# A long convolution by Fourier transforms: 32-bit pair copies of x on VectorE ahead of the first transform

## The chip, the core and the metric

The kernel runs on one core of a Trainium2 chip. The core has five engines, each with its own instruction queue: TensorE (PE; its weight loads are listed apart as PEld), VectorE (DVE), ScalarE (ACT), GpSimd (POOL) and SyncE (SP, which here only issues DMAs). They share an on-chip memory of 128 partitions (SBUF) and an accumulator memory (PSUM) that TensorE writes to. The metric is the device time of one execution in microseconds. A profile of one execution gives every instruction's start and duration.

## The reference

Inputs are x (8 x 5696 x 128), a filter h (5696 x 128) and four weight matrices. The first part is a causal convolution of every channel with its own filter, by real Fourier transforms of twice the length; the second mixes tokens and channels.

```python
Xf = np.fft.rfft(x, n=2*S, axis=1)
Hf = np.fft.rfft(h, n=2*S, axis=0)
y  = np.fft.irfft(Xf * Hf[None], n=2*S, axis=1)[:, :S, :]
theta = y @ w_theta
zr, zi = y * np.cos(theta), y * np.sin(theta)
u = y + einsum('ts,bsd->btd', w_tok_r, zr) + einsum('ts,bsd->btd', w_tok_i, zi)
out = u + np.maximum(u @ w_ch, 0.0)
```

The kernel's transforms work in float16.

## The kernel before

**Two parts.** The convolution takes the first 420 us or so; the token mixing, large matrix products with weights streamed in and transposed by VectorE (L714, L1099), takes the rest. The change lies in the first part alone.

**The transforms.** The length 11392 is split as 178 x 64, a sequence as 89 x 64. x of two batches sits in one tile `x16` (L125): partition = one of 89 blocks of 64 time steps, and within a partition 2 batches x 64 steps x 128 channels of float16, channels innermost. So the 128 values (2 x 64) of one channel lie 256 bytes apart. There are eight groups (L369): four pairs of batches, each in two halves `dh` of 64 channels. A group passes through four stages, all on TensorE, whose results are drained from PSUM by another engine:

- Stage A (L185 to L202), the first transform, one channel at a time. The weights that are loaded are the 89 x 128 values of the channel, `lhs(q)`, and the moving operand is a table of 89 x 180. Four channels make a chunk (one PSUM buffer); ScalarE drains it (L201) into the tile `a_`. A group has 16 chunks A.
- Stage B (L294 to L316): `f2` multiplies with the table `w_t2` (L212), ScalarE converts (L310, `xs`), and VectorE multiplies with the filter's spectrum twice (L312, into `u_t` and `v_t`). 12 chunks. In the last one, `f2` also issues 12 matmuls that no result needs (L218), into the same PSUM buffer.
- Stage C (L318 to L337): 16 matmuls a chunk, weights from `u_t` and `v_t` (L328, L329). VectorE drains the first half of a group's chunks and every second one of the rest (L336, into `g_`), ScalarE the others (L333, L334). 16 chunks. Each chunk reads all frequencies, so the first C of a group needs the last L312.
- Stage D (L339 to L366): back to time (L351), ScalarE drains (L354).

**What runs beside what.** `woven` (L222) merges lists of chunks by a position between 0 and 1 (L615): the 16 chunks C of a group are interleaved with the 16 chunks A of the next. Where the next group is the second half of the same batch pair (dh 1), the A lie in the first 0.35, three A to a C; where it is a new pair (dh 0), they lie in the first 0.55, one or two A to a C. Then come B of the next group and D of this one, interleaved (L621). All chunks take their PSUM buffer from one ring of four (L95), in program order, so that a chunk can start only when the fourth chunk before it has been drained. `x16` has one buffer: the load of the next pair (L130, 16 DMAs from GpSimd's queue) starts when the last A of the present one has read it.

**The first group.** Before it, tables are built on GpSimd (L150, L152), VectorE (L155, L156, L163, L182) and ScalarE (sines, L160, L167), among them `w_t2`, beside the transform of h, whose weights come from a tile `h16` with 128 bytes between values. The A of group 0 run alone, while the same engines build `r_u`, `r_v`, `sgn` and `e_t`.

**Order.** Each engine runs its instructions in the order that a scheduler fixed when the program was built; it can move an instruction ahead of others written earlier, where its tiles allow that.

Of the kernel before, what the change touches and what calls it, by code (L numbers as in the profile page):

```python
# [10 lines left out]
F32 = mybir.dt.float32  # L11
BF16 = mybir.dt.bfloat16
F16 = mybir.dt.float16
add = mybir.AluOpType.add
mult = mybir.AluOpType.mult
AF = mybir.ActivationFunctionType
ALU = mybir.AluOpType
# [5 lines left out]
def kernel(  # L23
# [10 lines left out]
    nc = tc.nc  # L34
    B, S, D = x.shape
    assert D == 128
    P = 128
# [39 lines left out]
    N2 = 64  # L77
    N1 = NF // N2
    NB = S // N2
    K1 = N1 // 2 + 1  # L80
    CK = 8
    HD = D // 2
# [7 lines left out]
    UVW = 2 * HD * K1  # L90
    hf_hbm = nc.dram_tensor("hf_hbm", (2, NCK, N2, 2, HD * CK), F16, kind="Internal").ap()
    yt_hbm = nc.dram_tensor("yt_hbm", (D, B, S), BF16, kind="Internal").ap()
# [4 lines left out]
    def psum():  # L97
        return fp.tile([P, 2, 512], F32, tag="ps", name="ps")

    conv, setup, xa, xin, pha = (ExitStack() for _ in range(5))  # L100

    def pool(name, bufs, stack, **kw):
        return stack.enter_context(tc.tile_pool(name=name, bufs=bufs, **kw))

    fa = pool("fft_a", 1, xa)
    fh = pool("fft_h", 4, xa)
    fx = pool("fft_x", 1, xin)
    NE, WB, BT = 9, 6 * 4 * CJ * 64, 7 * 1024
    keep = pool("keep", 1, ctx, side="right")
    fc = pool("fft_c", 1, conv, side="right")  # L110
# [3 lines left out]

    u_t = fc.tile([P, UVW + P], F16)
    v_t = fc.tile([P, UVW + P], F16)
    uv = [t[:, :UVW].rearrange("p (e d k) -> p e d k", e=2, k=K1) for t in (u_t, v_t)]
    h16 = s1.tile([P, 2, N2, HD], F16)
    for p0, p1 in ((0, 80), (80, NB)):
# [4 lines left out]
    def load_x(bp):  # L124
        x16 = fx.tile([P, 2, N2, D], F16, tag="x16", name="x16")  # L125
        for e in range(2):
            src = x[2 * bp + e]
            for n0 in range(0, N2, 16):
                for p0, p1 in ((0, 80), (80, NB)):
                    nc.gpsimd.dma_start(  # L130
                        x16[p0:p1, e, n0:n0 + 16, :].rearrange("p n d -> p (n d)"),
                        bass.AP(tensor=src.tensor, offset=src.offset + (p0 * N2 + n0) * D,
                                ap=[[N2 * D, p1 - p0], [1, 16 * D]]))
        return x16
# [8 lines left out]
    def turns_of(pattern, base, lanes, m, per, quarter=None):  # L143

        n = 1
        for _, c in pattern:
            n *= c
        t = s2.tile([P, 11 * NB], F32, tag="turn", name="turn")[:m, :n]
        k = s2.tile([P, 11 * NB], F32, tag="whole", name="whole")[:m, :n]
        nc.gpsimd.iota(k, pattern=pattern, base=base, channel_multiplier=0,  # L150
                       allow_small_or_imprecise_dtypes=True)
        nc.gpsimd.tensor_scalar(t, k, lanes, 1.0 / per, op0=mult, op1=mult)  # L152
        if quarter is not None:
            quarter(t)
        nc.vector.tensor_scalar(k, t, MAGIC, None, op0=add)  # L155
        nc.vector.scalar_tensor_tensor(t, k, MAGIC, t, op0=ALU.subtract, op1=ALU.subtract)  # L156
        return t, k
# [10 lines left out]

    f1_t = fc.tile([P, 2 * K1], F16)
    t, k = turns_of([[1, K1]], 0, lane[:NB, 1:2], NB, N1)  # L170
# [14 lines left out]
    def stage_a(lhs, both=False):  # L185

        st = {}

        def chunk(q):
            if q == 0:  # L190
                st["a"] = fa.tile([P, 2 * K1, HD], F16, tag="a", name="a_")
            ps = psum()
            for i in range(4):
                nc.tensor.matmul(ps[:, i // 2, (i % 2) * 2 * K1:(i % 2 + 1) * 2 * K1], lhs(q + i), f1_t[:NB],  # L194
                                 start=True, stop=True)
            a_out = st["a"][:, :, q:q + 4].rearrange("p k (a q) -> p k a q", a=2)
            a_in = ps[:, :, :4 * K1].rearrange("p a (q k) -> p k a q", q=2)
            if both and q % 8:
                nc.vector.tensor_copy(a_out, a_in)
            else:  # L200
                nc.scalar.activation(a_out, a_in, AF.Copy)  # L201
        return [lambda q=q: chunk(q) for q in range(0, HD, 4)], st  # L202
# [30 lines left out]
    x16s = {0: load_x(0)}  # L233
    steps, a_h = stage_a(lambda q: h16[:NB].rearrange("p h n d -> p (h n) d")[:, :, q], True)
# [59 lines left out]
    def stage_b(a_st, dh):  # L294

        hs_of = {}

        def load(c):
            if c >= NCK:
                return  # L300
            hs = hs_of[c] = fh.tile([P, 2, HD * CK], F16, tag="hs", name="hs")
            for e in range(2):
                nc.sync.dma_start(hs[64 * e:64 * e + 64], hf_hbm[dh, c])

        def chunk(c):
            c0, ck = CHK[c]
            hv = hs_of[c].rearrange("p r (d k) -> p r d k", k=CK)
            ps = f2(a_st, c)
            xs = fs.tile([P, 2, HD, CK], F16, tag="xs", name="xs")
            nc.scalar.activation(xs[:, :, :, :ck], ps, AF.Copy)  # L310
            for r in range(2):
                nc.vector.tensor_tensor(  # L312
                    uv[r][:, :, :, c0:c0 + ck], xs[:, :, :, :ck],
                    hv[:, r:r + 1, :, :ck].to_broadcast([P, 2, HD, ck]), op=mult)
            load(c + LEAD)
        return [lambda c=c: load(c) for c in range(LEAD)], [lambda c=c: chunk(c) for c in range(NCK)]  # L316
# [54 lines left out]
    def front(g):  # L371
        if g >= len(groups):
            return [], [], []
        bp, dh = groups[g]
        x16 = x16s[bp].rearrange("p b n d -> p (b n) d")
        steps, a_st = stage_a(lambda q: x16[:NB, :, dh * HD + q])
        return (steps, *stage_b(a_st, dh))

    a0, load0, b0 = front(0)
    woven(a0, [lambda: r_table(0, r_u), lambda: r_table(1, r_v), s_table] + load0)  # L380
    woven(b0, [lambda n0=n0: e_table(n0) for n0 in range(0, EN, 11)])
# [220 lines left out]
    for g, (bp, dh) in enumerate(groups):  # L602
        st = {}
        last = g + 1 == len(groups)
        a_, load_, b_ = front(g + 1)
        if last:
            for _ in range(3):
                steps0.pop(0)()
        now = [with_load(steps0.pop(0), n < 6) for n in range(9)] if last else []
        c_ = stage_c(st, last)  # L610
        if dh == 0 and bp + 1 < B // 2:
            def next_x(bp=bp):
                x16s[bp + 1] = load_x(bp + 1)
            a_ = a_ + [next_x]
        woven((c_, 0.06 if a_ else 0.0, 1.0), (a_, 0.0, 0.35 if dh == 0 else 0.55), now, load_)  # L615
        if g + 2 == len(groups):
            xin.close()
            open_phases()
            load_ya0()
        now = [steps0.pop(0) for _ in range(5)] if last else []  # L620
        woven(b_, (stage_d(st, bp, dh, load_ya1 if last else None), 0.0, 1.1 if b_ else 1.0), now)  # L621
        if g + 2 == len(groups):
            load_ya1()
            open_ring()
# [56 lines left out]
    bp = cp = wlp = ybp = None  # L681
# [248 lines left out]
    for i, (k, p, tt, j0, s0, nj) in enumerate(stretches):  # L930
# [38 lines left out]
        if tt is None:  # L969
            if p:  # L970
                aside(True, False)
            if first_of_pair:
                q = M1 if p else M3
# [4 lines left out]
            for j in range(nj):  # L978
                jj = j0 + s0 + j
                for r in range(2):  # L980
                    b = [x[:, r, :] for x in bts[jj]]
# [12 lines left out]
            if end_of_pair:  # L994
# [5 lines left out]
                c, c0 = c_last  # L1000
# [161 lines left out]
```

## Time and profile before

| | |
|---|---|
| Median of three runs | 2102.5 us (2101.66 to 2104.44) |
| The profiled execution | 2099.89 us |
| Its span, first to last instruction | 2098.1 us |
| Mean granted clock of TensorE | 0.978 |

Times below are within the span. The busy times of the first stages, from the table of busy time by stretch, in us:

| Stretch | What runs | PE | DVE | ACT | clock |
|---|---|---|---|---|---|
| 0 to 54.5 | tables, transform of h | 24.2 | 38.2 | 26.9 | 0.85 |
| 54.5 to 66.1 | A of group 0 | 9.5 | 9.1 | 10.9 | 0.79 |
| 66.1 to 88.4 | B of group 0 | 16.3 | 21.3 | 20.2 | 0.64 |
| 88.4 to 110.4 | C of group 0, A of group 1 | 22.0 | 14.2 | 14.4 | 0.92 |
| 110.4 to 131.1 | B of group 1, D of group 0 | 16.3 | 16.9 | 18.0 | 1.00 |
| 131.1 to 152.4 | C of group 1, A of group 2 | 21.2 | 14.4 | 17.6 | 1.00 |
| 345.5 to 368.5 | C of group 6, A of group 7 | 22.9 | 14.2 | 15.2 | 0.86 |
| 520 to 2098 | token mixing | 1547.9 | 1211.6 | 289.4 | 1.00 |

A row of the groups of instructions reads: line, engine, operation, what is written <- what is read, size, count | busy us in total, mean ns of one | idle us of the engine just before them and what ended most of it. A row of the timeline reads: start, duration, engine, line, operation, tiles, sizes, count, and in brackets the idle time before it with what ended it. Matmuls overlap each other, so their spacing, not their duration, is their cost.

### The profile page before, as it was taken

How to read it: one execution, taken by the hardware profiler on the slowest of the kernel's cores; microseconds unless marked ns; L12 is line 12 of the kernel's file. 1: busy time of each engine (PE TensorE's matmuls, PEld its weight loads, DVE VectorE, ACT ScalarE, POOL GpSimd, SP SyncE). 2: the span in 40 equal slices, each digit the busy share in tenths (PEclk: the TensorE clock that was granted, in tenths of full speed). 3: DMA queues.
4: the chain of work that ended last, by engine and by line, in shares of the span. 5: the costliest groups of instructions: out<-in, count | busy, mean ns of one | idle time of the engine just before them, and what ended most of it. 6: DMA issues, size and time to landing. Idle time of an engine off the chain costs nothing.

```text
span 2098.1 us, 41505 instructions
## 1 busy us (share of the span) xinstructions
PE 1979.5 (94%) x15688; PEld 1109.4 (53%) x15865; DVE 1595.2 (76%) x2881; ACT 675.3 (32%) x995; POOL 912.5 (43%) x1662
## 2 busy tenths in 40 slices
PE   4888999878999999999999999899999999999998
PEld 3788888754444444444444444344444444444444
DVE  7777776776878888888886766886777777777867
ACT  5887877874332333333310000011111111111111
POOL 5301010327444636354557554435354545445450
PEclk8799999989999999999999999999999999999999
DMA  7357474989989989898999989869797887879693
GB/s 144 94 137 175 123 171 121 239 243 239 179 153 179 178 175 168 171 173 177 171 175 152 154 167 284 136 107 156 127 154 132 148 142 136 154 130 155 126 155 89
DMA packets 408233, 334.97 MB, mean 160 GB/s; under 512 B 85895, under 2 KB 358407, under 8 KB 407047
## 3 DMA queue, kind: packets, MB, share of 16 engines
q0 software_dynamic: 225952, 156.72, 52.8%
q1 hardware_dynamic: 176096, 164.05, 27.3%
q10 hardware_dynamic: 5984, 11.54, 1.6%
q8 instruction: 124, 2.03, 0.4%
q14 instruction: 77, 0.63, 0.1%
HBM read 377.11 MB, written 92.49 MB: 224 GB/s over the span
## 4 chain that ended last, share of the span: by engine, by line
PE 63%; DVE 4%; DMA 2%; issue 2%; POOL 0%; ACT 0%; DVEq 0%
PE m L1099 59%; DVE c L1106 2%; DMA ring<-in_moe_w_tok_r_dram 1%; DVE b L655 1%; PE v L801 1%; PE utp L794 1%; PE m L1103 1%; DVE wt L714 1%; PE tpz L742 0%; PE theta_ps L396 0%; POOL ring L509 0%; PE m L986 0%; DMA yT<-yt_hbm 0%; PE m L1020 0%; DMA zl<-zl_hbm 0%
## 5 line engine op out<-in xcount | busy, mean ns | idle before, releaser
L509 POOL DMA_DIRECT2D ring<-in_moe_w_tok_i_dram x720 | 390.8, 557 | 653.0 <-DVE wt L714 579.6
L509 POOL DMA_DIRECT2D ring<-in_moe_w_tok_r_dram x720 | 389.0, 559 | 145.8 <-DVE wt L714 85.5
L714 DVE STREAM_TRANSPOSE wt<-ring 128x384 f32<-128x384 f32 (+2 forms) x720 | 359.3, 523 | 110.3 <-PE m L1099 70.0
L1099 PE MATMUL m<-b,wt 128*128 128x512 bf16 x1599 | 385.9, 380 | 4.1 <-DVE wt L714 1.7
L1099 PEld LDWEIGHTS <-wt 128*128 128x128 bf16 x1804 | 176.4, 98 | 219.7 <-DVE wt L714 7.8
L1106 DVE TENSOR_TENSOR c<-c,m 128x512 f32<-128x512 f32 x412 | 265.2, 669 | 0.4 <-PE m L1099 0.4
L796 ACT ACTIVATE ring<-utp 128x512 bf16<-128x512 bf16 x85 | 50.8, 597 | 582.3 <-PE utp L794 582.3
L328 PE MATMUL ps<-r_u,u_t 128*128 128x128 f16 x1024 | 126.4, 223 | 6.4 <-ACT red L419 3.0
L329 PE MATMUL ps<-r_v,v_t 128*128 128x128 f16 x1024 | 125.5, 223 | 0.4
L1020 PE MATMUL m<-b,wt 128*128 128x512 bf16 x466 | 110.2, 381 | 8.9 <-DMA b<-z_hbm 4.9
L791 ACT ACTIVATE ub<-c 128x512 bf16<-128x512 f32 x88 | 55.0, 628 | 191.5 <-DMA ring<-in_moe_w_tok_r_dram 113.0
L130 POOL DMA_DIRECT2D x<-in_x_dram x64 | 33.9, 536 | 184.9 <-PE ps L194 174.8
L328 PEld LDWEIGHTS <-u_t 128*128 128x128 f16 x1024 | 103.4, 101 | 5.5 <-DVE u_t L312 4.6
L329 PEld LDWEIGHTS <-v_t 128*128 128x128 f16 x1024 | 102.4, 100 | 4.4 <-issue 2.4
L310 ACT ACTIVATE xs<-ps 128x1024 f16<-128x1024 f32 x96 | 96.6, 1030 | 14.7 <-DVE v_t L312 6.7
L312 DVE TENSOR_TENSOR u_t<-xs,hs 128x1024 f16<-128x1024 f16 x96 | 68.6, 715 | 29.2 <-ACT xs L310 19.0
L1020 PEld LDWEIGHTS <-wt 128*128 128x128 bf16 x528 | 51.1, 99 | 69.2 <-issue 9.6
L194 PE MATMUL ps<-f_t,x 89*128 89x180 f16 x512 | 77.2, 298 | 4.0 <-ACT xs L310 2.6
L212 PEld LDWEIGHTS <-w_t 64*128 64x128 f16 x3240 | 60.8, 102 | 37.5 <-issue 24.5
L398 ACT ACTIVATE red<-theta_ps,magic 128x512 f32<-128x512 f32 (+1 forms) x46 | 31.6, 687 | 134.6 <-PE theta_ps L396 104.5
L194 PEld LDWEIGHTS <-x 89*128 89x128 f16 x512 | 70.8, 241 | 5.5 <-issue 4.5
L744 ACT ACTIVATE ring<-tpz 128x512 bf16<-128x512 bf16 (+1 forms) x46 | 27.5, 597 | 131.9 <-PE tpz L742 113.0
(2895 smaller groups left out, 3868.9 us busy)
## 6 DMA issues: line engine op xcount, KB each, us to landing
ring<-in_moe_w_tok_r_dram POOLq DMA_DIRECT2D x352, 96.0 KB, 4.5
ring<-in_moe_w_tok_i_dram POOLq DMA_DIRECT2D x352, 96.0 KB, 4.9
ring<-in_moe_w_tok_r_dram POOLq DMA_DIRECT2D x352, 80.0 KB, 4.5
ring<-in_moe_w_tok_i_dram POOLq DMA_DIRECT2D x352, 80.0 KB, 3.9
hs<-hf_hbm SPq DMA_DIRECT2D x192, 128.0 KB, 3.1
cp_hbm<-c SPq DMA_DIRECT2D x88, 256.0 KB, 2.5
c<-cp_hbm SPq DMA_DIRECT2D x88, 256.0 KB, 4.4
out_dram<-c SPq DMA_DIRECT2D x88, 256.0 KB, 4.5
```

Of the source, the lines that this page charges most:

```text
L194: nc.tensor.matmul(ps[:, i // 2, (i % 2) * 2 * K1:(i % 2 + 1) * 2 * K1], lhs(q + i), f1_t[:NB], start=True, stop=True)
L212: nc.tensor.matmul(ps[:, e, j * HD:(j + 1) * HD], w_t2[rows, c0 + j, N2 * (1 - ri):N2 * (3 - ri)], a_st["a"][rows, ri * K1 + c0 + j, :], s ...
L310: nc.scalar.activation(xs[:, :, :, :ck], ps, AF.Copy)
L312: nc.vector.tensor_tensor(uv[r][:, :, :, c0:c0 + ck], xs[:, :, :, :ck], hv[:, r:r + 1, :, :ck].to_broadcast([P, 2, HD, ck]), op=mult)
L328: nc.tensor.matmul(o, u_t[:, at:at + P], r_u, start=True, stop=False)
L329: nc.tensor.matmul(o, v_t[:, at:at + P], r_v, start=False, stop=True)
L509: nc.gpsimd.dma_start(wb[32 * i:32 * i + 32, :ng, :nj * 64], bass.AP(tensor=a.tensor, offset=a.offset + row0 * S + p * H + i * QR + j0 * 6 ...
L714: nc.vector.transpose(wt.rearrange("p j t r -> p (j t r)").bitcast(F32).rearrange("p (j g t) -> p g j t", j=TJ, g=4)[:, :ng, :nj], wb[:, : ...
L791: nc.scalar.activation(ub[:m].rearrange("p b d -> p (b d)"), c[:m], AF.Copy)
L1020: nc.tensor.matmul(ms[n // 2 * 2 + h], a[n][:, j, :, r], bts_of[p][jj][n % 2 * 2 + h][:, r, :], start=(n % 2 == 0 and jj == 0 and r == 0), ...
L1099: nc.tensor.matmul(ms[q], a[q][:, j, :, r], bts[jj][q][:, r, :], start=(jj == 0 and r == 0), stop=(jj == NJ - 1 and r == 1 and q not in left))
L1106: nc.vector.tensor_tensor(c, z, ms[q], op=op)
```

## The change

A chunk A no longer loads its weights from `x16`. For every eight channels, VectorE copies them first, as 32-bit words that each hold two neighbouring channels: a new tile `xt` of 4 pairs x 128 columns x 2 channels, so that the 128 words of a pair lie side by side. The copy is a bitwise or with 0 on words (89 x 512), from words 256 bytes apart into adjacent ones. A weight load then reads every second float16 of a pair's 128 words, 4 bytes apart. `xt` has two buffers of 2 KB a partition in a new pool. Eight copies serve the 16 chunks A of a group; eight groups make 64. The transform of h is as before.

```diff
+U32 = mybir.dt.uint32
...
     fx = pool("fft_x", 1, xin)
+    fxt = pool("fft_xt", 2, xin)
...
         bp, dh = groups[g]
-        x16 = x16s[bp].rearrange("p b n d -> p (b n) d")
-        steps, a_st = stage_a(lambda q: x16[:NB, :, dh * HD + q])
+        x32 = x16s[bp].rearrange("p b n d -> p (b n d)").bitcast(U32).rearrange("p (c d) -> p d c", d=HD)
+        side = {}
+
+        def cols(q):
+            if q % 8 == 0:
+                side["xt"] = xt = fxt.tile([P, 4, 2 * N2, 2], F16, tag="xt", name="xt")
+                at = (dh * HD + q) // 2
+                nc.vector.tensor_scalar(xt[:NB].rearrange("p d c r -> p (d c r)").bitcast(U32).rearrange(
+                    "p (d c) -> p d c", d=4), x32[:NB, at:at + 4], 0, None, op0=ALU.bitwise_or)
+            return side["xt"][:NB, q % 8 // 2, :, q % 2]
+        steps, a_st = stage_a(cols)
         return (steps, *stage_b(a_st, dh))
```

In the built program the copies stand on VectorE as follows: the first two of group 0 between two drains of h (L246) and the next table step (L155), the other six between the steps L155, L156 and L163 of the `e_t` table; the first two of a new pair between the L312 of the B before; the first two of a second half between the last drains L336 of the C stage before that; and the rest between the drains L336 of the C stage, mostly one to a drain. Each waits for TensorE to have read the buffer that it writes.

## The prediction

> **What bounds the kernel now.** First I read the busy shares by slice and by stage: from about 520 us to the end TensorE is busy 98%, and the change touches nothing there; only the first 370 us hold line L194. What happens there shifts all that follows, so a microsecond won on the path of the transforms is a microsecond of the whole. Then I read the groups of instructions for L194 and for loads of other layouts.
>
> ```profile
> L194 PE MATMUL ps<-f_t,x 89*128 89x180 f16 x512 | 77.2, 298 | 4.0 <-ACT xs L310 2.6
> L194 PEld LDWEIGHTS <-x 89*128 89x128 f16 x512 | 70.8, 241 | 5.5 <-issue 4.5
> L328 PEld LDWEIGHTS <-u_t 128*128 128x128 f16 x1024 | 103.4, 101 | 5.5 <-DVE u_t L312 4.6
> L1099 PEld LDWEIGHTS <-wt 128*128 128x128 bf16 x1804 | 176.4, 98 | 219.7 <-DVE wt L714 7.8
> ```
>
> A load from x steps 256 bytes between columns and takes 241 ns; u_t is contiguous (101), wt steps 4 bytes (98). The new buffers step 4 bytes, as wt does. Next, busy time by stretch, where one chunk A is 4 pairs of L194 and one chunk C 16 pairs of L328/L329.
>
> ```profile
> 131.06:145.13 14.07, 14.00 (x181) 13.87 (x182) 9.87 (x9) 12.35 (x14) 0.00 (x0) 1.00 0.58 152
> 94.59:99.56 4.97, 4.97 (x59) 4.87 (x56) 2.96 (x3) 4.62 (x7) 0.00 (x0) 1.00 0.01 3
> ```
>
> Columns: length, then busy time of PE, PEld, DVE, ACT, POOL, then clock. In the timeline, matmuls of C follow each other by 55 ns, so C is 16 x 0.055 = 0.89 us; twelve of L194 take 1.56 us (93.03 to 94.59), so A is 0.52 us. The first stretch (next group's dh 0, 8 C and 13 A) sums to 13.9 of 14.07: TensorE bound. The second is two cycles of one C and three A, 2.49 each where 0.89 + 1.56 = 2.45 is work, and the drains say that another loop ties with it:
>
> ```profile
> 93.23 1.50 DVE L336 TENSOR_TENSOR g__1380<-ps,sgn 90x1024 f16<-90x1024 f32 x1 [1.46 <-PE ps L329]
> 95.68 1.47 DVE L336 TENSOR_TENSOR g__1380<-ps,sgn 90x1024 f16<-90x1024 f32 x1 [0.94 <-PE ps L329]
> 98.21 1.41 DVE L336 TENSOR_TENSOR g__1380<-ps,sgn 90x1024 f16<-90x1024 f32 x1 [1.06 <-PE ps L329]
> ```
>
> With four PSUM buffers and four chunks to a cycle, the next C takes the buffer of this one: C 1.09 to its last result, drain 1.45, next C at 97.12 and 99.56. Faster loads alone win almost nothing there. Last, the seam of two groups:
>
> ```profile
> 128.10 0.69 DVE L312 TENSOR_TENSOR u_t<-xs,hs 128x1024 f16<-128x1024 f16 x1
> 128.69 1.35 ACT L310 ACTIVATE xs<-ps 128x256 f16<-128x256 f32 x1 [0.62 <-PE ps L218]
> 128.71 2.00 DVE L312 TENSOR_TENSOR v_t<-xs,hs 128x1024 f16<-128x1024 f16 x1
> 128.76 1.94 PE L194 MATMUL ps<-f_t,x 89*128 89x180 f16 x12
> 130.54 0.47 DVE L312 TENSOR_TENSOR u_t<-xs,hs 128x256 f16<-128x256 f16 x1
> 130.83 0.47 DVE L312 TENSOR_TENSOR v_t<-xs,hs 128x256 f16<-128x256 f16 x1
> 131.06 0.10 PEld L328 LDWEIGHTS <-u_t 128*128 128x128 f16 x1 [0.51 <-DVE u_t L312]
> ```
>
> The same product takes 0.69 us before L194 starts and 2.00 beside it, and C waits for it. Over the conversion stage the L312 of 128x1024 that lie over half beside L194 on x average 1.53 us (11 of them), the others 0.69 (161); L336 averages 1.39 beside it, 1.21 away from it; L310 of 128x256 0.94 against 0.40. I read this as the wide-stepped loads holding up whoever else reads or writes on-chip memory.
>
> **The change part by part.** Each group's 16 chunks A get 8 copies of 89 x 512 words on VectorE, 64 in all; the order of the other engines in the built program is the old one but for one swap of two chunks A with a C and the place of two GpSimd loads of ya0. No DMA is added.
>
> *Price of a copy.* No row has this operation. Below: L155, a tensor_scalar of 960 words in 0.65 us, gives 512 x 0.65 / 960 = 0.35. Above: L156 at 960 in 1.16 gives 0.62 at one word a cycle, and if the wide step costs it what it costs the loads (0.130 / 0.055 = 2.4 times) 1.46. I take a pitch of 0.50 and a row of 0.58: L194's load reads 128 columns at this very step in 0.130 us, 1.0 ns each, times 512, and a VectorE row overlaps the next by some 0.07 (L336 lasts 1.22 where five take 5.74). It is the row nearest in its access.
>
> The Trainium skill, Vector Engine (DVE) Microarchitecture Reference, 5.2 Measured stream behaviour on trn2, speaks against the copy: a stream that hops every element costs about 1.73 ns a column where a contiguous one costs 1.05. By that a copy would be an estimated 0.96 us at one word a cycle, and the sum below would come out near zero; at two words a cycle 0.52, and the sum would stand. No run here shows which.
>
> *Chunks A.* 180 columns at the pace of C: 0.055 x 180 / 128 = 0.077, so A falls from 0.52 to 0.31 us.
>
> *First group, a loss.* Its first two copies stand on VectorE ahead of L155 at 35.86 and wait for x, whose last DMA was issued at 28.7 and landed 8.2 us later, 36.9. So 1.0 wait + 2 x 0.50 = 2.0 us; behind them is the table chain L155, L156, w_t, L212, which TensorE waits for to 49.02. Then copy 3 stands behind an L155 that waits for GpSimd:
>
> ```profile
> 56.88 7.34 POOL L152 TENSOR_SCALAR turn<-whole,lane 90x979 f32<-90x979 f32 x2
> 60.85 1.75 DVE L155 TENSOR_SCALAR whole<-turn 90x979 f32<-90x979 f32 x1 [2.14 <-POOL turn L152]
> ```
>
> GpSimd's chain begins after the sgn of L290 and so moves 2.0 too. If it keeps its pace, L155 starts at 62.6; L155, L156, L163 and copies 4 to 8 then alternate, and the last drain of A (0.67 each) ends at 71.5 against 66.04: 5.4. If GpSimd too is freed (its second L150 would then take 1.11 as at 68.16, not 1.86), 3.2. I take 4.3 with the 2.0 in it. Bounds with the copy's: 2.7 to 9.
>
> *Seams, a gain.* If L312 goes back to 0.69 and L310 to 0.40, each seam's chain L218, L310, L312, C is rewritten: at 131.06 C starts at 129.95 and its first chunk no longer waits halfway, 1.35; the seven, in order: 1.7, 1.35, 1.7, 1.1, 1.45, 1.0, 1.4 = 9.7 us. Bounds 0 (the slowness has another cause) to 9.7. The two copies between L312s there fall in VectorE gaps of 0.2 to 0.7 us; x has landed some 4 us before (last issue 111.2 + 7.0 against 122.3). Without that cover they cost 1.0 at three seams.
>
> *dh 1 next (four groups), three A to a C.* Drain at 1.21 to 1.25, C 1.09: the loop is 2.30, and one or two copies (0.5, 1.0) fit in the 1.09 in which VectorE waits for C. ScalarE needs 3 x 0.70 = 2.1, below that. Four cycles x 0.15 x 4 groups = 2.4 gained; 0 if drains stay 1.45.
>
> *dh 0 next (three groups).* TensorE falls to 8 x 0.89 + 13 x 0.31 = 11.2; VectorE becomes the bound: 8 drains + 6 copies = 8 x 1.21 to 1.30 + 3.0 = 12.7 to 13.4 from the end of the first C (1.05), less 1.8 since two more C need no drained buffer: 12.0 to 12.7 against 14.07. I take 1.7 each, 5.1.
>
> *Sum:* +4.3 - 9.7 - 2.4 - 5.1 = -12.9 us. The profiled execution took 2099.9 (span 2098.1), the median of the runs is 2.6 above it at 2102.5; so 2087 for a profile, **2090 us** for the runs.
>
> **The rivals.**
>
> *Copy too dear (slower).* At a pitch of 1.30: first group +9; seams -9.7; dh 1 next, VectorE has 1.3, 2.6, 1.3 between drains where 1.09 is free: 3 x 1.23 + 5.2 = 8.9 against 7.4, +1.5 x 4 = 6; dh 0 next 8 x 1.21 + 7.8 + 1.05 - 1.8 = 16.7, +2.7 x 3 = 8. Together +13: 2116 us. Linear between both prices it decides from a pitch of about 0.9. For it: the step costs the loads 2.4 times. Against: a load reads fewer bytes a word. Chance 0.2.
>
> *No relief, no gain.* The slow L312 and L336 have another cause, or the copies, which read with the same step, cause it again. Then +4.3, seams 0, dh 1 next 0, dh 0 next 8 x 1.32 + 3.0 + 1.05 - 1.8 = 12.8, -1.3 x 3 = -4: 2103. For it: beside h, whose loads step 128 bytes, L155 keeps 0.65, so not every stepped load does it; in the first group the slow L155 and L156 (1.75 and 2.63) lie beside GpSimd as well. Against: at the seams GpSimd is idle. Chance 0.2.
>
> *The loads stay slow.* 4-byte steps with 89 rows could cost 241 ns again: then only the losses, about 2106. Against: wt, 98 ns. Chance 0.03.
>
> *The clock.* TensorE with more idle time could lose clock (the last three columns are clock, DMA share, GB/s):
>
> ```profile
> 343.00:344.00 1.00, 0.16 (x2) 0.16 (x2) 1.00 (x3) 0.62 (x2) 0.00 (x0) 1.00 0.33 115
> 347.00:348.00 1.00, 1.00 (x10) 1.00 (x9) 0.33 (x1) 0.00 (x0) 0.00 (x0) 0.50 1.23 318
> ```
>
> After two such idle microseconds the clock was 0.50 from 345 to 351.4, which cost some 3 us of TensorE's time; at all seven seams that is +21, so 2111. Against: TensorE would be busy 1.83 of 2.30, 80%, and between 110.4 and 131.1 it was busy 16.3 of 20.7 at a clock of 1.00; and shorter seams leave it less idle there. Chance 0.07. The Trainium skill, TensorE: Matmul & The Clock Gate, Part 1, has the clock halve after a window of about 3.4 us that counts as idle; it doesn't say from which share on, so these rows decide.
>
> **How the numbers follow.** My forecast has 0.5, the rivals 0.2, 0.2, 0.03 and 0.07. Its own range is 2082 to 2098: the seams at seven tenths, VectorE's drains at 1.30, the first group at its bounds. The two larger rivals reach to 2103 and 2116; up to 2110 leaves out about the dearest half of the copy's rival and a part of the clock's, and below 2082 lies what a copy of 0.35 us would win on top: 8 chances in 10 for 2082 to 2110. A change of 0.2%, 4.2 us, is about what a measurement of this kernel can tell from none. Faster than 2098.3: nearly all of the forecast and the cheap edges of two rivals, 0.56. Within: most of the second rival, and copies near the price where the sum is zero, 0.19. Slower: 0.25.
>
> **What would show it.** L194's loads near 98 ns and its matmuls 0.08 us apart, or the loads stay. The copy's row: 0.35 to 0.6 us as forecast, over 0.97 and it turns. L312's longest near 0.7 and L310 of 128x256 near 0.40 at the seams, L336 near 1.21 in all: the relief; as before: none. Between the first and the ninth C where the next group has dh 0, VectorE, no longer TensorE, is busy nearly throughout. The last drain of the first A at some 70 us instead of 66. I would be wrong above all if copies of 256-byte steps disturb the others as the loads did, since two thirds of the gain hang on that.

## The result and the profile after

The changed kernel takes 2084.3 us (median of six runs, 2082.4 to 2086.1) where the kernel before takes 2102.1 us (six runs, 2096.5 to 2105.5): a ratio of 0.992, 95% interval 0.991 to 0.993. Forecast were 2090 us. The profiled execution took 2084.2 us, its span is 2082.4. The last C ends at 419.5 us before and at 402.9 after, 16.6 us earlier, and 15.7 of that are left at the end of the span, so the gain is made in the transforms and passes on nearly whole.

Up to the copy (L384) the lines of the changed kernel stand two further down than before: L194 is now L196, L312 is L314, L336 is L338. First the groups of instructions, for the rows shown before:

```profile
L196 PE MATMUL ps<-f_t,xt 89*128 89x180 f16 x512 | 54.4, 250 | 9.1 <-DVE xt L384 6.5 <-ACT xs L312 1.1 <-ACT yt L356 0.3
L196 PEld LDWEIGHTS <-xt 89*128 89x128 f16 x512 | 42.0, 102 | 14.0 <-DVE xt L384 9.8 <-issue 3.5 <-DVE whole L165 0.2
L330 PEld LDWEIGHTS <-u_t 128*128 128x128 f16 x1024 | 100.7, 98 | 6.7 <-DVE u_t L314 6.0 <-DVE ring L593 0.8
L384 DVE TENSOR_SCALAR xt<-x 89x512 uint32<-89x512 uint32 x64 | 46.9, 751 | 0.0
```

The loads fell from 241 to 102 ns, and TensorE now waits for copies in places (6.5 us before matmuls, 9.8 before loads). A copy has a row of 0.75 us. Next the seam into group 1, the one that the prediction showed (VectorE, then TensorE, by start and duration):

```profile
125.03 1.42 DVE L384 TENSOR_SCALAR xt<-x 89x512 uint32<-89x512 uint32 x2
126.37 0.68 DVE L314 TENSOR_TENSOR u_t<-xs,hs 128x1024 f16<-128x1024 f16 x1
130.54 0.69 DVE L314 TENSOR_TENSOR u_t<-xs,hs 128x1024 f16<-128x1024 f16 x1 [0.43 <-ACT xs L312]
131.15 0.69 DVE L314 TENSOR_TENSOR v_t<-xs,hs 128x1024 f16<-128x1024 f16 x1
131.75 0.39 DVE L314 TENSOR_TENSOR u_t<-xs,hs 128x256 f16<-128x256 f16 x1
130.43 1.09 PE L196 MATMUL ps<-f_t,xt 89*128 89x180 f16 x12
132.20 0.23 PE L330 MATMUL ps<-r_u,u_t 128*128 128x128 f16 x1 [0.68 <-DVE u_t L314]
```

Beside the twelve L196 the product L314 keeps 0.69 us, where it took 2.00; and the twelve take 1.09 where they took 1.94 here. But two copies, 1.34 us until the next product starts, now stand among the products; that product's input was ready at 125.81, 0.56 us before it started. The stretch with dh 0 next and two cycles with dh 1 next, as the prediction showed them, and the engines in such a cycle:

```profile
132.20:145.00 12.80, 11.92 (x177) 10.93 (x178) 12.35 (x15) 9.62 (x14) 0.00 (x0) 1.00 0.69 182
94.13:98.58 4.45, 3.97 (x57) 3.68 (x57) 4.22 (x6) 4.19 (x7) 0.00 (x0) 1.00 0.24 68
```

```profile
95.22 1.22 DVE L338 TENSOR_TENSOR g__1403<-ps,sgn 90x1024 f16<-90x1024 f32 x1 [0.23 <-PE ps L331]
95.53 2.10 ACT L203 ACTIVATE a__1374<-ps 128x720 f16<-128x720 f32 x3
96.36 0.22 PE L330 MATMUL ps<-r_u,u_t 128*128 128x128 f16 x1 [0.24 <-ACT a__1374 L203]
96.36 1.40 DVE L384 TENSOR_SCALAR xt<-x 89x512 uint32<-89x512 uint32 x2
```

In the stretch with dh 0 next VectorE (the third busy time) is busy 12.35 of 12.80 us and TensorE 11.92, which speaks for VectorE as the bound; experiment 3 tests it. In the cycles of one C and three A, two take 4.45 us, 2.23 each, where they took 2.49. What is left is a loop through TensorE and ScalarE: C takes 0.89 us, the first A is drained from 0.51 after its start on, that drain lasts 0.77, and the next C, which waits for it, starts 0.05 later, 2.22 in all. ScalarE is busy 2.10 of them and waits 0.13 for TensorE. Drains L338 last 1.22.

The stages, read from TensorE's timeline (first C matmul to last; seam: from there to the next first C), for the two kernels and the runs that are told below, in us:

| | before | after | group 0 direct | 32-word copies | longer A | six of eight wide | step 272 | by column |
|---|---|---|---|---|---|---|---|---|
| start of the first C | 88.4 | 91.6 | 88.8 | 87.2 | 93.6 | 95.6 | 88.5 | 89.0 |
| seven seams | 147.2 | 139.0 | 138.3 | 137.7 | 140.4 | 148.5 | 151.3 | 140.4 |
| four C, dh 1 next | 89.1 | 80.1 | 81.1 | 80.9 | 84.1 | 88.4 | 80.1 | 80.1 |
| three C, dh 0 next | 64.1 | 62.2 | 62.0 | 56.4 | 66.1 | 64.1 | 56.2 | 58.3 |
| last C | 30.8 | 29.9 | 29.0 | 29.7 | 29.8 | 29.9 | 31.6 | 28.5 |
| median of the runs | 2102.1 | 2084.3 | 2083.5 | 2077.7 | 2096.6 | 2106.9 | 2088.9 | 2083.0 |
| its own before | | 2102.1 | 2101.3 | 2101.3 | 2102.7 | 2102.7 | 2102.7 | 2102.5 |

Before to after: first C +3.3, seams -8.1, C with dh 1 next -9.0, C with dh 0 next -2.0, last C -0.8: -16.6 at the end of the last C.

### The profile page after: what moved, and what is told of

The parts are those of the page before. It is cut to its first block, busy times and chain, and to the rows that moved or that the text cites. A ratio compares the mean times of both kernels' runs of the same rounds, so it can differ in the third digit from the quotient of the medians.

```text
span 2082.4 us, 41613 instructions
## 1 busy us (share of the span) xinstructions
PE 1954.7 (94%) x15688; PEld 1076.5 (52%) x15865; DVE 1618.3 (78%) x2945; ACT 659.0 (32%) x995; POOL 901.1 (43%) x1662
## 3 DMA queue, kind: packets, MB, share of 16 engines
q1 hardware_dynamic: 176096, 164.05, 27.2%
## 4 chain that ended last, share of the span: by engine, by line
PE 63%; DVE 4%; DMA 3%; issue 2%; POOL 1%; ACT 0%; DVEq 0%; POOLq 0%
PE m L1110 59%; DMA ring<-in_moe_w_tok_r_dram 2%; DVE c L1117 1%; DVE b L666 1%; PE v L812 1%; PE utp L805 1%; DVE wt L725 1%; PE m L1114 1%; POOL ring L520 1%; PE tpz L753 0%; PE theta_ps L407 0%; PE m L997 0%; PE m L1031 0%; DMA zl<-zl_hbm 0%; DMA wl<-in_moe_w_tok_i_dram 0%
## 5 line engine op out<-in xcount | busy, mean ns | idle before, releaser
L312 ACT ACTIVATE xs<-ps 128x1024 f16<-128x1024 f32 x96 | 91.5, 979 | 10.9 <-DVE v_t L314 6.7
L314 DVE TENSOR_TENSOR u_t<-xs,hs 128x1024 f16<-128x1024 f16 x96 | 64.8, 675 | 28.9 <-ACT xs L312 20.3
L409 ACT ACTIVATE red<-theta_ps,magic 128x512 f32<-128x512 f32 (+1 forms) x46 | 31.6, 687 | 135.2 <-PE theta_ps L407 112.2
L431 ACT ACTIVATE mag<-mag,half_pi 128x512 f32<-128x512 f32 (+1 forms) x90 | 65.5, 728 | 0.0
L314 DVE TENSOR_TENSOR v_t<-xs,hs 128x1024 f16<-128x1024 f16 x96 | 63.5, 661 | 0.0
```

The source lines that it names most:

```text
L314: nc.vector.tensor_tensor(uv[r][:, :, :, c0:c0 + ck], xs[:, :, :, :ck], hv[:, r:r + 1, :, :ck].to_broadcast([P, 2, HD, ck]), op=mult)
L431: nc.scalar.activation(mag, mag, AF.Sin, bias=half_pi[:m], scale=-TWO_PI)
```

## The experiments

### 1. Group 0 without copies

```diff
-        steps, a_st = stage_a(cols)
+        if g == 0:
+            x16 = x16s[bp].rearrange("p b n d -> p (b n) d")
+            steps, a_st = stage_a(lambda q: x16[:NB, :, dh * HD + q])
+        else:
+            steps, a_st = stage_a(cols)
```

> Group 0 alone loads its weights directly from x16 again, as the kernel before did; groups 1 to 7 keep their copies. Theory: the eight copies of group 0 are a pure loss, because they stand on VectorE ahead of and between the table steps L155, and there the first C came at 91.6 us instead of 88.4. Without them the first C should start at 87.5 to 89 and the whole should take 2079 to 2082 us, against 2084.3 for the changed kernel. Rival: the first group's later C has another cause (the order of the table steps or a half clock in that stretch), then the time stays at 2083 to 2086.

Measured: 2083.5 us, ratio 0.9915 (0.9898 to 0.9932); the profiled execution 2081.2, first C at 88.8. 2.8 us come back, but not all copies left the first group: where the two ahead of L157 stood, the build put the first two of group 1. VectorE's timeline in the changed kernel, then in this run:

```profile
28.60 2.78 DVE L184 TENSOR_SCALAR w_t<-w_t 128x960 f16<-128x960 f16 x1
37.83 1.38 DVE L384 TENSOR_SCALAR xt<-x 89x512 uint32<-89x512 uint32 x2
39.13 0.65 DVE L157 TENSOR_SCALAR whole<-turn 128x960 f32<-128x960 f32 x1
```

```profile
36.45 1.39 DVE L384 TENSOR_SCALAR xt<-x 89x512 uint32<-89x512 uint32 x2 [0.95 <-DMA x<-in_x_dram]
37.75 0.66 DVE L157 TENSOR_SCALAR whole<-turn 128x960 f32<-128x960 f32 x1
```

The table step L157 (before: L155 at 35.86) starts 3.3 us later in the changed kernel and 1.9 later here. What the run takes out are the other six copies, between the steps of the `e_t` table: from its first matmul to the start of its last, A of group 0 takes 13.1 us in the changed kernel, 9.3 here and 9.3 before. But the median of the whole is only 0.8 below the changed kernel's, and the intervals overlap: that this version is faster isn't settled.

### 2. Copies that nothing reads

```diff
-            return side["xt"][:NB, q % 8 // 2, :, q % 2]
+            return x16[:NB, :, dh * HD + q]
```

> All 64 copies are made, but chunks A load their weights from x16 as before, so nothing reads the copies. Theory (the gain comes from the weight loads no longer stepping 256 bytes, the copies are pure cost): the long L312 (1.5 us on average beside L194, up to 2.0) and the long L336 (1.4) are back, and the copies add their 0.65 each where VectorE has no room: 2104 to 2113 us, slower than the kernel before (2102). Rival (the gain comes from something else that the change brought with it, such as the order of the chunks or where copies stand): 2082 to 2092.

Measured: 2130.6 us, ratio 1.0137 (1.0120 to 1.0155), dearer than the theory had it. A miss in its design: with no reader, the copies wait for nothing but their input, so the build moved them ahead. In the seam into group 1, sixteen copies run from 133 to 150 us, ten of them among the last products, and the three seams into groups 1, 3 and 5 take 25.4 to 26.7 us instead of 20.6 to 22.5. It shows what copies cost where all else waits for VectorE, not what the loads are worth. Experiment 5 does that.

### 3. Copies of 32 words

```diff
...
-    "p (d c) -> p d c", d=4), x32[:NB, at:at + 4], 0, None, ...
+    "p (d c) -> p d c", d=4)[:, :, :8], x32[:NB, at:at + 4, :8], 0, None, ...
```

The other words of `xt` are zeros, so this kernel leaves most of x out of the result.

> Each copy moves 32 of its 512 words; the other weights of the first transform are zeros, so most of the input x is left out of the result. Everything else, loads of weights with a step of 4 bytes included, is as in the changed kernel. Theory (the copies at 0.65 us still cost in three places: the first group, the seams into groups 1 and 7, and the three C stages with a new pair next, where VectorE became the bound): 2071 to 2078 us, first C about 89, the three stages with dh 0 next shorter by 1.5 to 3 us each. Rival (copies lie in idle time of VectorE everywhere but in the first group): 2080 to 2082. A caution for both: zeros as weights could change the granted clock.

Measured: 2077.7 us, 23.5 below its own before; the changed kernel stands 17.8 below its own. So the copies at full length cost some 5.7 us. A copy takes 0.18 us here. The table says where the cost lies: 4.4 at the first C, 5.8 in the three stages with dh 0 next (18.8 each, where the changed kernel has 20.4, 20.4 and 21.4), 1.3 in the seams, and none with dh 1 next. It says where more surely than how much: its differences come to 11.0 at the end of the last C, of which 7.5 are left at the end of the span and 5.7 between the medians. The rival, hidden everywhere but in the first group, falls.

### 4. A longer A without wide loads

Each matmul of A for x is followed by one of 120 columns, so that A costs TensorE what it did before. In a first form the second matmul asked for copies of its own.

```diff
+                w = lhs(q + i)
...
+                if not both:
+                    nc.tensor.matmul(ps[:, i // 2, 4 * K1:4 * K1 + 120], w, f1_t[:NB, :120],
+                                     start=True, stop=True)
```

> As the changed kernel, but each matmul of chunk A for x is followed by one more, of 120 columns, whose result nothing reads, so that a chunk A takes TensorE 0.50 us again (0.128 a matmul pair) as with the wide-stepped loads, while all loads step 4 bytes. Theory (most of the gain is the relief of VectorE and ScalarE from the wide-stepped loads, the smaller part TensorE's own shorter A): L312 stays at 0.69 and L336 at 1.21, the loop of one C and three A goes back to 2.45 (+0.22 x 4 x 4 = 3.5 us) and the three stages with dh 0 next get about 1 us each longer, in all 2088 to 2093. Rival (the gain is TensorE's shorter A, the engines' shorter rows follow from that or are worth nothing): 2100 to 2106.

Measured in the first form: 2160.0 us, ratio 1.0272 (1.0245 to 1.0300). It made 128 copies, two for each pair of chunks, and with two buffers none was ready ahead: TensorE's matmuls waited 45 us for copies. It says nothing of the question. The second form has the 64 copies and the changed kernel's order on TensorE and ScalarE; on VectorE a few copies stand a product or two elsewhere:

> The run with a longer chunk A once more, now with the 64 copies of the changed kernel: one copy serves both matmuls of a channel (in the run before, the second matmul asked for copies of its own, 128 in all). Each matmul of chunk A for x is followed by one of 120 columns that no result needs, so A takes TensorE about 0.50 us again while all loads step 4 bytes; the order on all engines is that of the changed kernel. Theory (most of the gain is relief of VectorE and ScalarE): L314 stays at 0.69 and L338 at 1.22, the loop of one C and three A is 2.45 again, in all 2088 to 2094 us. Rival (the gain is TensorE's shorter A): 2100 to 2106.

Measured: 2096.6 us, ratio 0.9972 (0.9961 to 0.9982), between the theory's 2088 to 2094 and the rival's 2100 to 2106. Groups, and ScalarE's timeline:

```profile
L200 PE MATMUL ps<-f_t,xt 89*128 89x120 f16 x512 | 75.9, 222 | 0.0
L388 DVE TENSOR_SCALAR xt<-x 89x512 uint32<-89x512 uint32 x64 | 47.1, 748 | 3.3 <-PE ps L200 2.5 <-DMA x<-in_x_dram 0.8
```

```profile
97.92 2.10 ACT L207 ACTIVATE a__1438<-ps 128x720 f16<-128x720 f32 x3 [0.40 <-PE ps L200]
100.37 2.10 ACT L207 ACTIVATE a__1438<-ps 128x720 f16<-128x720 f32 x3 [0.36 <-PE ps L200]
```

Three chunks A take 1.56 us on TensorE, as before the change, products and drains stay short (L318 0.69, L342 1.22), and the cycle is 2.46 us again: TensorE is its bound, and ScalarE waits for it. So TensorE's shorter A alone is worth 11.7 us (17.8 below before against 6.1), 4.0 of them in the stages with dh 1 next, some 4 in those with dh 0 next (one of them beside a half clock, a granted clock of 0.50, from 136 to 139 us, worth about 1.5), the rest at the seams and before the first C.

### 5. Six of eight channels from x16

```diff
+            if q % 8 in (0, 7):
+                return side["xt"][:NB, q % 8 // 2, :, q % 2]
+            return x16[:NB, :, dh * HD + q]
```

> As the changed kernel, copies and order too, but of the eight channels of a copy only the first and the last load their weights from it; the other six load from x16 with the step of 256 bytes. So the copies stand where they did (which they did not in the run in which nothing read them: there 13 of a pair's copies ran ahead into one seam). Theory (wide-stepped loads hold up VectorE and ScalarE): the long L314 and L338 are back for three quarters, the copies' cost stays, 2100 to 2111 us. Rival (relief is worth little): A costs TensorE 0.47 us against 0.31, as in the run with the longer A, 2087 to 2093.

Measured: 2106.9 us, ratio 1.0017 (1.0007 to 1.0028), as the theory had it. The copies stand where they did, A is no longer than in experiment 4 (three chunks 1.50 us at a full clock, 1.56 there), but three loads of four step 256 bytes. The long product is back at the place shown above:

```profile
138.81 1.65 DVE L314 TENSOR_TENSOR u_t<-xs,hs 128x1024 f16<-128x1024 f16 x1 [0.42 <-ACT xs L312]
```

and L312 of 128x256 averages 0.66 us on ScalarE (0.41 in the changed kernel). Against experiment 4 the time is 10.3 us longer: that is what the wide loads do to the others, at three quarters of their number, half clocks included (below 0.75 in 27 of the 320 stretches of 1 us from 90 to 410 us, against 4 in experiment 4). So the change's gross gain is made of two parts of like size, about 12 us from TensorE's own shorter A and 10 to 14 (10.3, or 10.3 x 4 / 3) from the relief of VectorE and ScalarE, and the copies take about 6 back; 12 + 12 - 6 is the 18 measured. How much of either part is the clock's these runs don't separate.

### 6. Is it the step of 256 bytes?

```diff
-        x16 = fx.tile([P, 2, N2, D], F16, tag="x16", name="x16")
+        x16 = fx.tile([P, 2, N2, D + 8], F16, tag="x16", name="x16")
...
-                        x16[p0:p1, e, n0:n0 + 16, :].rearrange("p n d -> p (n d)"),
+                        x16[p0:p1, e, n0:n0 + 16, :D],
...
```

> The kernel before, without copies, with 16 bytes of padding behind the 128 channels, so that chunks A load their weights with a step of 272 bytes instead of 256; the DMAs of x then write pieces of 256 bytes. Theory (any step this wide is slow and holds up the other engines): loads near 240 ns, L312 long beside them, 2098 to 2108 us, more if x lands later. Rival (it is the step of exactly 256 bytes): loads near 100 ns, L312 at 0.69, and without copies 2072 to 2080 us, unless x lands too late for the seams.

Measured: 2088.9 us, ratio 0.9933 (0.9916 to 0.9949): neither range. The groups decide for the rival:

```profile
L194 PEld LDWEIGHTS <-x 89*128 89x128 f16 x512 | 44.6, 145 | 7.2 <-issue 6.7
```

The loads take 145 ns, A's pace is 0.078 a matmul (twelve in 1.10), L312 averages 0.69 and L336 1.22, with no copy at all; the three stages with dh 0 next take 56.2 us, as with copies of 32 words. Of the steps tried here, that of exactly 256 bytes is the one that holds the loads up and makes them hold up others. The gain is lost at three seams of 24.3, 22.3 and 25.5 us, into which the next pair's x lands in pieces of 256 bytes. There VectorE waits for DMAs of hs (17.6 us in the first 430, against 8.4 before), and TensorE stops within a chunk that waits for nothing:

```profile
112.79 0.81 PE L212 MATMUL ps<-a__1355,w_t 64*128 64x64 f16 x43
116.62 0.49 PE L212 MATMUL ps<-a__1355,w_t 64*128 64x64 f16 x21 [3.02 <-issue]
117.05 1.02 PE L351 MATMUL ps<-e_t,g__1380 90*128 90x89 f16 x20
```

43 of 64 matmuls of one chunk, 3.02 us of nothing, then the other 21; after it the clock is 0.50 to 128 us. The kernel before stops at the same matmul, only for less long:

```profile
117.76 0.48 PE L212 MATMUL ps<-a__1355,w_t 64*128 64x64 f16 x21 [2.18 <-issue]
```

Instructions come by DMA too: the profile has a queue of kind "instruction" (q8), with packets of 16 KB about every 5 us here. The one before this stop starts at 113.98, 2.64 us ahead of the matmul at 116.62; in the kernel before it is 115.19 and 117.76, 2.57 us. From 90 to 400 us the kernels before and after and all the runs told here have 49 stops of TensorE of 0.8 us or more without a visible wait, and each ends 2.2 to 3.2 us after the start of such a packet. So TensorE was most likely waiting for instructions there. Why they came later with the padding isn't shown, but the DMA engines were busier: in the seam into group 1 the packets' time adds up to 1.08 of that of 16 engines, against 0.74 before and 0.61 in the changed kernel, for no more bytes a second (171, 182 and 161 GB/s).

### 7. A step of 264 bytes, and hs two chunks earlier

```diff
+    fh2 = pool("fft_h2", 2, xin)
...
-        x16 = fx.tile([P, 2, N2, D + 8], F16, tag="x16", name="x16")
+        x16 = fx.tile([P, 2, N2, D + 4], F16, tag="x16", name="x16")
...
+        LEAD = 6 if more else 4
...
+            hs = hs_of[c] = (fh2 if more and c % 3 == 2 else fh).tile(...)
```

> The kernel before without copies, with 8 bytes of padding behind the 128 channels (weight loads step 264 bytes) and six instead of four buffers of hs, two of them in the pool stack of x, for groups 1 to 6. In the run with 272 bytes the seams into groups 1, 3 and 5, in which the next pair's x lands in pieces of 256 bytes, took 24.3, 22.3 and 25.5 us where the changed kernel takes 20.5, 19.9 and 20.0, with VectorE waiting for DMAs of hs. Theory (only exact multiples such as 256 bytes are held up; hs loaded two chunks earlier rides over x's traffic): loads near 145 ns, L312 at 0.69, those three seams near 20.5 to 22, 2077 to 2084 us. Rivals: a step of 264 is held up as 256 is, 2095 or more; or the bandwidth itself is short, seams stay at 22 to 25 and the time at 2086 to 2091.

Measured: 2089.6 us, ratio 0.9938 (0.9920 to 0.9955). The loads take 157 ns at this step, L312 stays at 0.69, and VectorE's wait for hs falls to 2.3 us in the first 430 (with 272 bytes: 17.6). But the three seams take 25.9, 24.0 and 27.2 us: TensorE stands still there for 3.8 us at a time (before 117.4 and 201.3) with no wait that the profile shows, and half clocks follow. Both stops end some 3 us after an instruction packet has started (114.42 and 198.16), and in the first of these seams the packets' time adds up to 1.30 of the 16 engines'. So more buffers take away the wait for hs and not the long seams. That speaks for the rival about the DMAs, in their time rather than in bytes (164 GB/s); no run tests it alone.

### 8. Copies on GpSimd

Group 0 direct, group 1 copied by VectorE, the others by GpSimd.

```diff
+                if g < 2:
+                    nc.vector.tensor_scalar(out, x32[:NB, at:at + 4], 0, None, op0=ALU.bitwise_or)
+                else:
+                    nc.gpsimd.tensor_copy(out.bitcast(F32), x32[:NB, at:at + 4].bitcast(F32))
```

> The changed kernel, with group 0 loading directly from x16, group 1 copied by VectorE and groups 2 to 7 copied by GpSimd (a copy of the words as float32), which is idle there but for the DMAs of x. Theory (the copies cost the seam into group 1 and the three stages with dh 0 next, where VectorE is the bound; GpSimd's copies take 1 to 1.9 us and fit eight times into a stage of 20 us): 2076 to 2081 us, drains L338 at 1.22. Rival (GpSimd's copies with a wide step hold up VectorE as TensorE's loads did, or come too late for A): L338 and L314 longer, A waiting for copies, 2085 to 2100 us.

Measured: 2092.8 us, ratio 0.9950 (0.9934 to 0.9967): the rival's range. A copy takes 1.07 us. Two of the three C stages with dh 0 next reach 18.8 and 18.7, but products of the seams that meet a copy stand still for its length (GpSimd and VectorE, timeline):

```profile
167.03 1.11 POOL L388 COPY xt<-x 89x512 f32<-89x512 f32 x1 [23.55 <-PE ps L196]
167.15 1.54 DVE L314 TENSOR_TENSOR u_t<-xs,hs 128x1024 f16<-128x1024 f16 x1
169.02 1.17 POOL L388 COPY xt<-x 89x512 f32<-89x512 f32 x1 [0.89 <-PE ps L196]
169.21 1.24 DVE L314 TENSOR_TENSOR u_t<-xs,hs 128x256 f16<-128x256 f16 x1
```

Six of the seven seams are 20.7 to 21.6 us again. Drains L338, which read PSUM, stay at 1.22 beside the copies.

### 9. One drain more for ScalarE

Group 0 direct, and in three stages the seventh C drained by ScalarE.

```diff
-            if q % 16 == 0 and (last or q >= 64):
+            if q % 16 == 0 and (last or q >= (48 if new else 64)):
```

> The changed kernel with group 0 loading directly from x16 and, in the three C stages with a new pair next (groups 1, 3, 5), the seventh chunk's drain given to ScalarE. Theory (VectorE, with six copies and eight drains, bounds these stages from the first C to the ninth: 20.4 us, against 18.8 with copies of 32 words): each gets shorter by 0.8 to 1.3 us, 2077 to 2081 us. Rival (the bound there is ScalarE's or TensorE's as much): the stages stay near 20.4 and the time at 2081 to 2085, as in the run with group 0 direct alone (2083.5).

Measured: 2087.8 us, ratio 0.9925 (0.9905 to 0.9946), above both. The stages with dh 0 next take 21.4, 20.4 and 21.2 us, so nothing is won there; two of them hold a half clock. The one with a full clock settles it: it takes 20.4 as in experiment 1, though VectorE is busy 0.7 us less up to the tenth C (12.79 against 13.53). From C to C both stages lose most from the fifth to the eighth (1.79, 2.10 and 1.80 us), and taking the seventh C's drain from VectorE shortens none of these. The theory falls in this stage without the clock's help.

### 10. The copy by column

Group 0 direct; a copy takes the four words of a column together, and weight loads step 16 bytes.

```diff
-                xt = fxt.tile([P, 4, 2 * N2, 2], F16, ...)
+                xt = fxt.tile([P, 2 * N2, 8], F16, ...)
...
-                    "p (d c) -> p d c", d=4), x32[:NB, at:at + 4], 0, None, op0=ALU.bitwise_or)
+                    "p (c d) -> p c d", d=4), x32[:NB, :, at:at + 4], 0, None, op0=ALU.bitwise_or)
```

> The run with group 0 direct, but the other seven groups' copies walk in another order: the four words of a column together, then the next column 256 bytes on, and xt holds the eight channels of a column side by side, so weight loads step 16 bytes instead of 4. Theory (the copy's 0.74 us is the price of one word every 256 bytes, and VectorE bounds the C stages with a new pair next): the copy falls to 0.35 to 0.5 us, loads stay near 98 ns, those stages go from 20.4 to 19 to 19.7 us, in all 2077 to 2081 us. Rival (the price is that of the words, whatever their step): the copy stays at 0.7 and the time at 2081 to 2085, as in the run with group 0 direct (2083.5).

Measured: 2083.0 us (2078.5 to 2086.7), ratio 0.9911 (0.9894 to 0.9929); groups of the first 430 us:

```profile
L196 PEld LDWEIGHTS <-xt 89*128 89x128 f16 x448 | 38.6, 145 | 4.0 <-issue 3.7
L384 DVE TENSOR_SCALAR xt<-x 89x512 uint32<-89x512 uint32 x56 | 22.2, 415 | 1.8 <-DMA x<-in_x_dram 1.8
```

The same 512 words cost 0.41 us instead of 0.74, and two in a row 0.75 instead of 1.40: the price was that of hopping after every word. Two of the stages with dh 0 next fall to 18.9, the third (20.5) holds a half clock from 208 to 212 us. TensorE no longer waits for copies, and a load of 145 ns leaves A's pace at 0.078. By the profiled executions this is the fastest kernel that computes all (2078.5 against 2084.2), but its median is 1.3 us below the changed kernel's and the intervals overlap: that it beats it is likely by its stages, not settled by its time. The Trainium skill, Vector Engine (DVE) Microarchitecture Reference, 5.2 Measured stream behaviour on trn2, says that a stream keeps its full rate in runs of two or more adjacent 4-byte words that start on an 8-byte boundary, whatever the hop between runs; this agrees in kind (0.41 against 0.74).

## Why the prediction came out right

The sign and the size held, but not term by term: one gain was far too small (dh 1 next, 6.6 us) and one too large (dh 0 next, 3.1), and that they partly cancel is luck.

- **Loads and A.** Forecast 98 ns and 0.077 a matmul: measured 98 (median), and 0.077.
- **The copy.** Forecast a row of 0.58 and a pitch of 0.50, measured 0.74 and 0.65 (two in 1.40). The step that failed is taking TensorE's load, 1.0 ns a column at this step, for VectorE: it needs 1.27 ns a word. The prediction's estimates by the Trainium skill, Vector Engine (DVE) Microarchitecture Reference, 5.2 Measured stream behaviour on trn2, 0.96 us at one word a cycle and 0.52 at two, lie on both sides of the row. It stayed below the break-even pitch of 0.9, so that rival (0.2) fell.
- **First group.** Forecast +4.3, less the 1.7 of its own seam, so +2.6 at the first C; measured +3.3. The last drain of A ends at 71.2 instead of 66.05, 5.1 later (forecast some 70), and 1.9 come back in B. The two copies ahead of L157 were priced at 2.0 with their wait for x, and L157 starts 3.3 later. But only 1.3 of that are the copies themselves: they start at 37.83 because L184 at 28.60 took 2.78 us, where it took 0.41 before and at most 0.46 in the other runs with this order; why isn't shown. Where copies stand at this place in those runs they wait 0.8 to 1.9 us for x, and L157 starts 1.9 to 3.0 us later than before, so the price of 2.0 was at the low end.
- **Seams.** Forecast for the other six -8.0, measured -8.3 (groups 1 to 6), and +0.2 at the seventh. Relief came in full, but not seam by seam. The one into group 1 gained 0.1 instead of 1.35. Its two copies didn't fall in a gap (0.56 us of delay for the product behind them), and the clock is half from 121 to 124 us; in experiment 1, with the same two copies but a full clock there and a stop of TensorE of 1.31 us instead of 2.36, the seam gains 1.0. The seam into group 5 gained 2.5 instead of 1.0: the kernel before had a half clock there, from 290 to 297 us. So the sum is near by luck.
- **dh 1 next.** Forecast -2.4, measured -9.0: the largest miss. "Faster loads alone win almost nothing there" is wrong, and the step that failed is the one that leads to it: that the next C takes the buffer of this one and so waits for VectorE's drain. In the prediction's own lines the next C starts at 94.59, 97.12 and 99.56, each time before that drain has ended (94.73, 97.15, 99.62). What ends 0.05 us before each of these starts is ScalarE's drain of the first A (0.77, 0.86 and 0.77 us, to 94.54, 97.07 and 99.51), and the changed kernel's profile names it as what C waits for. ScalarE's timeline before, where the x3 and x4 start with these drains:

```profile
93.77 2.10 ACT L201 ACTIVATE a__1355<-ps 128x720 f16<-128x720 f32 x3 [0.76 <-PE ps L194]
96.21 3.29 ACT L201 ACTIVATE a__1355<-ps 128x720 f16<-128x720 f32 x4 [0.35 <-PE ps L194]
```

So VectorE's long drains held up nothing in these cycles, and both TensorE's own work (2.45) and the loop through ScalarE's drain got shorter with A. Experiment 4 agrees: with every drain at 1.22 but the long A, the cycle is still 2.46 instead of 2.23. The cycle gives 0.26 x 4 x 4 = 4.2; most of the rest is the half clock at the head of these stages, which is gone in all four. In stretches of one microsecond from 90 to 410 us the clock is below 0.75 in 23 of 320 before and in 7 after.
- **dh 0 next.** Forecast -5.1, measured -2.0. VectorE is the bound as forecast, busy 12.35 of 12.80. The term was mis-sized by the copy's price, 6 x 0.15 x 3 = 2.7 us, and the third stage holds a half clock. Experiment 3 shows that the copies were the bound there: without most of their price the term is -7.8.
- **No relief, no gain** (0.2) fell: experiment 5 brings the slow rows back with the wide loads alone. **The loads stay slow** and **the clock**: the rows fell to 98, and half clocks became fewer, not more.

So the forecast of 12.9 us became 17.8 because TensorE's own shorter A, which was thought nearly worthless with dh 1 next, is about half of the gain, while what was thought two thirds, the relief, is the other half. How much of either is the clock's isn't settled: the half clocks differ from one execution to the next.

## What to carry to other kernels

Look at the step at which weights are loaded: one of 256 bytes cost 241 ns a load here and slowed two other engines, and 16 bytes of padding (272) or a copy removed both. Before calling a gain worthless because another loop ties with it, look up in the timeline which drain the waiting chunk is released by: here it was ScalarE's drain of A, not VectorE's of C, and the cycle fell with A from 2.49 to 2.23. A copy that gathers should take several adjacent words at a time, and a fix that only changes a layout should be asked what it does to the DMAs that fill it.

## What the hardware showed that was not expected

- A load of 89 x 128 weights by its step: 98 ns at 4 bytes, 144 at 16, 174 at 128 (the transform of h), 241 at 256, 157 at 264, 144 at 272. Only that of 256 was seen to slow others: an all-float16 product on VectorE 0.69 to 2.00 us, ScalarE's drain of 128x256 0.41 to 0.81 on average in the kernel before (0.66 in experiment 5). The Trainium skill, SBUF — State Buffer, SBUF: two separate sides, says that within the engines only the port pair of VectorE and GpSimd contends and that TensorE, ScalarE and VectorE's own pair wait for no one; at this step the traces show otherwise, with GpSimd idle. Why 256 is special isn't shown.
- The same page, Who interferes with whom, lets a VectorE operation with two inputs in SBUF wait for a GpSimd operation that reads there. Experiment 8 agrees: 0.69 became 1.54 us beside a copy of 1.11, and drains from PSUM kept 1.22.
- TensorE can stand still within a chunk most likely because its instructions are late: 49 stops of 0.8 to 4.5 us, each ending 2.2 to 3.2 us after a 16 KB packet of the instruction queue started, in the kernel before too, and longest (3.0 to 4.5) where x lands in 256-byte pieces. Of the eleven stops of 1.9 us or more, ten are followed within 2 us by a half clock.
- Half clocks made single profiles differ by several microseconds: the granted clock is below 0.75 in 7 of 320 stretches of the changed kernel, 40 of 320 with the step of 264.
